# Eight stores to DRAM issued from GpSimd's queue instead of SyncE's, in a training step of an S4 convolution and a gated feed-forward layer

## The chip, the cores and the metric

The kernel runs on one core of a Trainium2 chip. The metric is the device time of one execution in microseconds (us). A kernel is executed several times and the median of its runs is quoted with the lowest and the highest. Ratios are computed as the mean time of one kernel's fast runs over that of the other's of the same rounds, so they are not quite the ratio of the medians that I quote. A run counts as slow when it is more than 1.5% above the fastest of the same kernel; slow runs are named where they matter. The kernel before was run on five different chips. Its medians ranged from 763.9 to 768.8 us and its single runs from 759.9 to 776.9 us (the last a slow run), so a difference of half a per cent between two kernels is not resolved. Each kernel was profiled once, in one of its runs, so stretches of two kernels are compared on one profile each.

## The reference

The function is a layer norm, a long convolution whose filter comes from a diagonal state-space model, a feed-forward layer, and a gate. The kernel computes the output and, for a given output gradient, the gradients of 11 inputs. Everything is bfloat16, with L = 2048 tokens, D = 512 channels, N = 128 states and F = 1792 hidden features.

```python
xn = _layernorm(x)
# _A_ref: K[d, l] = Re(sum_n C[d,n] * dB[d,n] * exp(l * dt[d] * A[d,n])), then an FFT convolution
s = irfft(rfft(xn, 2L) * rfft(K, 2L))[:L] + xn * Dskip
# _B_ref
o = silu(xn @ w1) @ w2
out = x + s * silu(o)
# outputs: out and the vjp of it for grad_out with respect to
# A_u, A_A_re, A_A_im, A_B_re, A_B_im, A_C_re, A_C_im, A_log_dt, A_Dskip, B_w1, B_w2
```

## The kernel before

Channels are handled in four blocks of 128 (`b` = 0 to 3). The FFT is done as two steps of matrix products with a transposing load, here called dB, between them. So each transform is a chain: TensorE, a copy on ScalarE, the transposing load (issued by SyncE), TensorE again.

```python
def dft_fwd(k, w8, U, ev, tag="w8"):
    # ... first step: TensorE products into ps, ev() casts them into A (dA) on ScalarE
    B = w8.tile([P, 2, 16, P], BF16, name="dB", tag=tag)
    nc.sync.dma_start_transpose(B[:]..., A[:]...)            # line 278: 1 MB, transposing
    for _ in range(LAG):
        yield                                                # other work is woven in here
    # ... second step: ps_s <- dB, F on TensorE (lines 287 and 288)
```

The backward stretch weaves three things: the transforms of the gradient, one block after the other; the feed-forward layer's gradient; and the output.

```python
def gen_ffn_da(k, da):
    for c in range(T // 2):                                  # 8 groups of 256 tokens
        dT = da.tile([P, 8, P], BF16, name="doT", tag="doT", bufs=2)
        nc.sync.dma_start_transpose(dT[:], k.do[...])        # line 845, "d o transpose"
        if c == 0:
            nc.sync.dma_start_transpose(k.W1T[:], k.ins["B_w1"])
        for f in range(FT // 2):
            if f in (0, 4):
                # ... slope <- Hd (line 855), Silu and Tanh on ScalarE, slope_less_one on VectorE
            # ... ps_da on TensorE; dh = (dh + 1) * ps_da on VectorE (line 867)
            if f in (3, 6):
                nc.sync.dma_start(k.DHd[...], dh[:, 0:n])    # line 870: store of d h, 512 or 384 KB
        for t in range(2):
            pd = da.tile([P, D], BF16, name="pd_s", tag="pd_s", bufs=1)
            # ... ps_dx on TensorE, cast on ScalarE
            nc.sync.dma_start(k.Pd[:, 2 * c + t, :], pd[:])  # line 879: store of partial d x, 128 KB
# gen_conv_bwd ends with
    nc.sync.dma_start(k.dUd[b], du[:]...)                    # line 648: store of d u
# gen_out stores the output from GpSimd already: k.st = nc.gpsimd.dma_start
```

The order in which each engine issues its instructions is not the order of this text. It is decided when the program is built, by a scheduler that works from its own idea of how long things take. Moving a store to another engine can therefore change the order of what comes later, on every engine. When the two programs are built and compared, TensorE, VectorE, ScalarE, GpSimd and SyncE all issue in another order, although the change touches no instruction of the first three.

Of the kernel before, what the change touches and what calls it, by code (L numbers as in the profile page):

```python
# [386 lines left out]
def gen_tables(k, b):  # L387

    nc, tbl = k.nc, k.tbl
    TT = nc.vector.tensor_tensor  # L390
    NX = NE + len(Y_EXP)
    Xr = tbl.tile([P, 4, NE, 32], BF16, name="Xr", tag="Xr")
    for h in range(2):
        hs = slice(b * P + 64 * h, b * P + 64 * h + 64)
        mag = tbl.tile([P, NX, 64], BF16, name="mag", tag="mag")
        nc.sync.dma_start(mag[:].rearrange("p e d -> p (e d)"), k.Md[2 * b + h])
        E = tbl.tile([P, 2, 16, NE, 4], BF16, name="E", tag="E", bufs=2)
        Y = k.Y[h]
        H = tbl.tile([P, 2, 16, 3, 4], BF16, name="H", tag="H")
        qe = lambda ap: ap.rearrange("p e (q a) -> p e q a", a=4)  # L400
        for (x0, n) in ((0, 8), (8, 8), (16, 5), (21, 7), (28, 3)):
            V = tbl.tile([P, 2, 8, 64], I32, name="V", tag="tv", bufs=2)
            TS = nc.vector.tensor_single_scalar
            TT(out=V[:, 1, 0:n], in0=k.tau[:, hs].unsqueeze(1).to_broadcast([P, n, 64]),
               in1=k.ecst[:, x0:x0 + n].unsqueeze(2).to_broadcast([P, n, 64]), op=ALU.mult)
            TS(out=V[:, 0, 0:n], in_=V[:, 1, 0:n], scalar=-float(1 << (PB - 2)), op=ALU.add)
            TS(out=V[:, :, 0:n], in_=V[:, :, 0:n], scalar=32 - PB, op=ALU.logical_shift_left)
            sn = tbl.tile([P, 2, 8, 64], BF16, name="sn", tag="ts", bufs=2)
            nc.scalar.activation(out=sn[:, :, 0:n], in_=V[:, :, 0:n], func=ACT.Sin, scale=-2 * PI_LO / 2.0 ** 32)
            for c in range(2):  # L410
                if x0 < NE:
                    segs = [(E[:, c, :, x0:x0 + n, :], 0, n)]
                else:
                    segs = [(Y[:, c, :, 1:8, :] if x0 == NE else H[:, c], 0, n)]
                for o, s0, s1 in segs:
                    TT(out=o.rearrange("p q e a -> p e q a"), in0=qe(sn[:, c, s0:s1]), in1=qe(mag[:, x0 + s0:x0 + s1, :]), op=ALU.mult)
            yield
        nc.sync.dma_start(k.Ed[b, h], E[:].rearrange("p c q e a -> p (c q e a)"))
        lo = lambda c: Y[:, c, :, 0:8, :].unsqueeze(2).to_broadcast([P, 16, 3, 8, 4])
        hi = lambda c: H[:, c].unsqueeze(3).to_broadcast([P, 16, 3, 8, 4])  # L420
        out = lambda c: Y[:, c, :, 8:32, :].rearrange("p q (k m) a -> p q k m a", m=8)
        shp = [P, 16, 3, 8, 4]
        for c, (x, y), op in ((0, ((0, 0), (1, 1)), ALU.subtract), (1, ((0, 1), (1, 0)), ALU.add)):
            m1 = tbl.tile(shp, BF16, name="m1", tag="tv", bufs=2)
            m2 = tbl.tile(shp, BF16, name="m2", tag="tm", bufs=1)
            TT(out=m1[:], in0=lo(x[0]), in1=hi(x[1]), op=ALU.mult)
            TT(out=m2[:], in0=lo(y[0]), in1=hi(y[1]), op=ALU.mult)
            TT(out=out(c), in0=m1[:], in1=m2[:], op=op)  # L428
        nc.sync.dma_start(k.Yd[b, h], Y[:].rearrange("p c q j a -> p (c q j a)"))
        yield  # L430
        for q0 in range(0, 16, 8):
            W = tbl.tile([P, 4, 8, NE, 4], BF16, name="W", tag="W", bufs=2)
            for m, (cm, ec) in enumerate(((0, 0), (1, 1), (2, 1), (1, 0))):
                d0 = hs.start + 4 * q0
                ct = k.CT[:, cm, d0:d0 + 32].rearrange("p (q a) -> p q a", a=4).unsqueeze(2).to_broadcast([P, 8, NE, 4])
                TT(out=W[:, m], in0=E[:, ec, q0:q0 + 8], in1=ct, op=ALU.mult)
            for u in range(2):
                ps = k.pt.tile([P, 4, 84], F32, name="ps_k", tag="pt")
                for q in range(4):
                    for m in range(4):  # L440
                        nc.tensor.matmul(out=ps[:, q], lhsT=Y[:, m // 2, q0 + 4 * u + q].rearrange("p j a -> p (j a)"),  # L441
                                         rhs=W[:, m, 4 * u + q].rearrange("p e a -> p (e a)"), start=(m == 0), stop=(m == 3))
                qq = 16 * h + q0 + 4 * u
                k.evk(Xr[:, :, :, qq:qq + 4], ps[:].rearrange("p q (e a) -> p a e q", a=4))
            yield

    def group(o, terms):
        n = len(terms) * 4
        i = 0
        for kind, e0, e1 in terms:  # L450
            for a in range(4):
                nc.tensor.matmul(out=o, lhsT=k.SEL[:, kind, a], rhs=Xr[:, a, e0:e1, :], start=(i == 0), stop=(i == n - 1))
                i += 1
    KE = tbl.tile([P, 8, 8, 32], BF16, name="KE", tag="KE")
    bc = lambda ap, n: ap.unsqueeze(2).to_broadcast([P, ap.shape[1], n, 32])
    ev = k.evk
    A = k.pt.tile([P, 16, 32], F32, name="ps_e", tag="pt")
    group(A[:], [(0, 0, 16)])
    ev(KE[:, 0], A[:, 8:16])
    ev(KE[:, 1:8, 0:2, :], bc(A[:, 0:7], 2))  # L460
    ev(KE[:, 2:8, 2, :], A[:, 1:7])
    ev(KE[:, 4:8, 3, :], A[:, 3:7])
    B = k.pt.tile([P, 16, 32], F32, name="ps_e", tag="pt")
    group(B[:, 0:5], [(0, 16, 21)])
    group(B[:, 5:12], [(1, 0, 7), (2, 1, 8)])
    group(B[:, 12:16], [(3, 3, 7), (2, 4, 8)])
    ev(KE[:, 1, 2, :], B[:, 0])
    ev(KE[:, 1, 3:6, :], B[:, 1:2].to_broadcast([P, 3, 32]))
    ev(KE[:, 1, 6, :], B[:, 2])
    ev(KE[:, 1, 7, :], B[:, 5])  # L470
    ev(KE[:, 2:4, 3:6, :], bc(B[:, 3:5], 3))
    ev(KE[:, 2:8, 6:8, :], bc(B[:, 6:12], 2))
    ev(KE[:, 4:8, 5, :], B[:, 8:12])
    ev(KE[:, 4:8, 4, :], B[:, 12:16])
    for a in range(4):
        nc.scalar.dma_start(k.Kd[b, a].rearrange("i j r -> j i r"), KE[a:P:4].rearrange("p i t q -> p i (t q)"))
    yield
# [8 lines left out]
def gen_conv_x(k, b):  # L486

    bs = slice(b * P, b * P + P)
    dft = k.dft
    U, _ = yield from dft_fwd(k, dft, lambda t: k.xn[:, t, bs], k.evc)  # L490
    k.nc.sync.dma_start(k.Ud[b], U[:].rearrange("p c g k -> p (c g k)"))
    yield


def gen_conv_fwd(k, b):

    nc, dft = k.nc, k.dft
    bs = slice(b * P, b * P + P)
    Kb = dft.tile([P, 4, 16, 32], BF16, name="Kb", tag="t4")
    nc.sync.dma_start(Kb[:].rearrange("p a t q -> p a (t q)"), k.Kd[b].rearrange("a i (r s) x -> (i r) a (s x)", s=2))  # L500
    for _ in range(LAG):
        yield
    KX, A2 = yield from dft_fwd(k, dft, lambda t: Kb[:, :, t, :], k.evc)
    U = spectrum_in(k, dft, b, "U")
    nc.sync.dma_start(k.KXd[b], KX[:].rearrange("p c g k -> p (c g k)"))
    yield
    cplx_mul(k, dft, KX, U)
    S = dft.tile([P, 16, P], BF16, name="S_b", tag="t4")

    def consume(t0, n, ps):  # L510
        xd = dft.tile([P, 8, P], BF16, name="xd", tag="cm2")
        nc.vector.tensor_tensor(out=xd[:], in0=k.xn[:, t0:t0 + n, bs], in1=k.Dbc[:, bs].unsqueeze(1).to_broadcast([P, n, P]), op=ALU.mult)
        nc.vector.tensor_tensor(out=S[:, t0:t0 + n], in0=ps[:], in1=xd[:], op=ALU.add)
    yield from dft_inv(k, A2, U, k.evc, consume)
    k.S_b = S
    nc.sync.dma_start(k.Sd[b], S[:].rearrange("p t d -> p (t d)"))
    yield


# [98 lines left out]
def gen_conv_bwd(k, b):  # L618
    nc, dft = k.nc, k.dftb
# [4 lines left out]
    U = spectrum_in(k, dft, b, "U")  # L624
    KX = spectrum_in(k, dft, b, "K")
# [15 lines left out]
    du = dft.tile([P, 16, P], BF16, name="du_b", tag="t4")  # L641
# [3 lines left out]
        TT(out=xd[:], in0=k.ds[:, t0:t0 + n, bs], in1=k.Dbc[:, bs].unsqueeze(1).to_broadcast([P, n, P]), op=ALU.mult)  # L645
        TT(out=du[:, t0:t0 + n], in0=ps[:], in1=xd[:], op=ALU.add)
    yield from dft_inv(k, A2, KX, k.evc, consume_dx)
    nc.sync.dma_start(k.dUd[b], du[:].rearrange("p t d -> p (t d)"))
    yield


# [187 lines left out]
def gen_ffn_da(k, da):  # L839
    nc = k.nc  # L840
    D, FT, DK, T = k.D, k.FT, k.DK, k.T
    W2T = k.W2T
    for c in range(T // 2):
# [6 lines left out]
        for f in range(FT // 2):  # L850
            if f in (0, 4):
                n = 8 if f == 0 else 6
                sl = da.tile([P, 8, 256], BF16, name="slope", tag="slope", bufs=2)
                dh = da.tile([P, 8, 256], BF16, name="dhT", tag="dhT", bufs=3)
# [12 lines left out]
            nc.vector.scalar_tensor_tensor(out=dh[:, i0:i0 + 2, :], in0=dh[:, i0:i0 + 2, :], scalar=1.0, in1=ps[:], op0=ALU.add, op1=ALU.mult)  # L867
            if f in (3, 6):
                f0, n = (0, 8) if f == 3 else (8, 6)
                nc.sync.dma_start(k.DHd[f0:f0 + n, :, 256 * c:256 * c + 256].rearrange("f p n -> p f n"), dh[:, 0:n])  # L870
            yield
        for t in range(2):
            pd = da.tile([P, D], BF16, name="pd_s", tag="pd_s", bufs=1)
# [2 lines left out]
                nc.tensor.matmul(out=ps[:], lhsT=dhs[ft // 8][:, ft % 8, t * P:t * P + P], rhs=k.W1T[:, ft, :],  # L876
                                 start=(ft == 0), stop=(ft == FT - 1))
            k.evb(pd[:], ps[:])
            nc.sync.dma_start(k.Pd[:, 2 * c + t, :], pd[:])
            yield  # L880


# [210 lines left out]
```

## Time and profile before

| Kernel before | |
|---|---|
| time, median (lowest to highest), 3 runs | 767.86 us (766.88 to 769.71) |
| span of the profiled run, mean granted TensorE clock | 767.7 us, 0.906 |
| first load of d o, the gate's input, issued (the forward part is nearly done) | 242.7 us |
| first d o transpose issued | 329.0 us |
| last store of d h issued | 519.9 us |
| first load for the weight gradients (GE) issued | 541.4 us |

The times of issue are read from the timeline and the line view of the trace. They cut the run into stretches that I use throughout: forward, the chain from the gate to the first d o transpose, the backward stretch from there to the last store of d h, and the rest.

The first lines are from the page of the kernel before: busy us of an engine, its share of the span and its instructions; then, for the two main DMA queues, packets, MB, and the share of 16 engines' time. q1 is fed by SyncE, q0 by GpSimd.

```profile
PE 581.8 (76%) x4987; PEld 405.3 (53%) x5036; DVE 547.6 (71%) x1110; ACT 494.9 (64%) x678; POOL 89.6 (12%) x167
...
DMA packets 262094, 167.32 MB, mean 218 GB/s; under 512 B 188816, under 2 KB 242064, under 8 KB 258192
...
q1 hardware_dynamic: 249056, 143.94, 74.1%
q0 software_dynamic: 6224, 18.10, 7.3%
```

No engine is full. (In the instruction counts a few TensorE records are missing from the trace.) The next lines are the kernel before by stretches: the window, its length, busy us and instruction count of each engine, granted clock, DMA share and GB/s.

```profile
core 0: us, PE busy (x) PEld busy (x) DVE busy (x) ACT busy (x) POOL busy (x), PEclk, DMA share, GB/s
50.00:245.00 195.00, 168.80 (x1520) 113.31 (x1539) 156.76 (x326) 159.45 (x241) 19.65 (x26) 0.95 0.81 234
245.00:335.00 90.00, 46.31 (x372) 31.94 (x374) 73.67 (x97) 50.38 (x65) 20.99 (x16) 0.77 0.90 258
335.00:515.00 180.00, 154.29 (x1234) 108.74 (x1246) 140.06 (x200) 128.22 (x128) 6.96 (x12) 0.95 0.82 224
```

TensorE is nearly full in the forward and backward stretches (169 of 195 us, 154 of 180 us) and half empty between them, where a chain of loads and gate arithmetic decides.

### The profile page before, as it was taken

To read this page: it belongs to the slowest core of one execution; us is meant where nothing else is said; L and a number is where in the kernel's file an instruction comes from. 1 tells how busy PE (TensorE), PEld (TensorE's weight loads), DVE (VectorE), ACT (ScalarE), POOL (GpSimd) and SP (SyncE) were. 2 spreads that over 40 slices of the span, in tenths; PEclk is the share of its full clock that TensorE was granted. 3 is DMA by queue.
4 is the path that set the end of the run, shared out by engine and by line. 5 is a ranking of instruction groups with operands and counts; after the bars stand their busy time and mean duration, and the time that the engine had idled before them with its cause. 6 is when DMAs were issued, how large, how long until landed. Compare 5 with 4: busy or idle time off the path is not lost. (4 is left out here: it accounts for less than half of the span.)

```text
span 767.7 us, 12970 instructions
## 1 busy us (share of the span) xinstructions
PE 581.8 (76%) x4987; PEld 405.3 (53%) x5036; DVE 547.6 (71%) x1110; ACT 494.9 (64%) x678; POOL 89.6 (12%) x167
## 2 busy tenths in 40 slices
PE   0579877888997616568887988995576877799995
PEld 0346653664763513356565575762263455488774
DVE  6979987685887985885796796877354293698620
ACT  6869767787998655476686587756365566474221
POOL 3020110010010351000000010001000002111220
PEclk9979988999999766999999899999589988899998
DMA  9988978499589759999969788289899999769373
GB/s 278 329 177 257 252 224 257 145 274 277 196 223 300 298 164 237 286 296 315 237 203 270 217 225 211 76 221 280 222 131 212 221 218 210 160 116 182 89 179 56
DMA packets 262094, 167.32 MB, mean 218 GB/s; under 512 B 188816, under 2 KB 242064, under 8 KB 258192
## 3 DMA queue, kind: packets, MB, share of 16 engines
q1 hardware_dynamic: 249056, 143.94, 74.1%
q0 software_dynamic: 6224, 18.10, 7.3%
q10 hardware_dynamic: 6752, 4.46, 2.0%
q8 instruction: 39, 0.64, 0.4%
q14 instruction: 23, 0.19, 0.1%
HBM read 58.06 MB, written 62.26 MB: 157 GB/s over the span
## 5 line engine op out<-in xcount | busy, mean ns | idle before, releaser
L42 ACT CAST dA<-ps_s 128x1024 bf16<-128x1024 f32 x96 | 94.3, 1030 | 37.7 <-PE ps_s L288 19.1
L537 PE MATMUL ps_h<-XT,W 128*128 128x256 bf16 x448 | 61.7, 289 | 32.2 <-DMA XT<-xn 25.3
L891 PE MATMUL ps_w<-do,a_tok 128*128 128x512 bf16 x215 | 60.3, 436 | 24.1 <-ACT a_tok L888 17.0
L537 PEld LDWEIGHTS <-W 128*128 128x128 bf16 x448 | 45.5, 104 | 43.4 <-issue 20.6
L717 DVE TENSOR_TENSOR Tp<-Vb,Eb 128x1344 bf16<-128x1344 bf16 x64 | 52.0, 852 | 20.4 <-PE psS L733 12.3
L300 PE MATMUL ps_i<-I,sp_in 128*128 128x256 bf16 x384 | 53.1, 285 | 16.1 <-DVE sp_in L323 9.4
L42 ACT CAST dB<-ps_i 128x1024 bf16<-128x1024 f32 x48 | 47.0, 1020 | 28.2 <-PE ps_i L300 22.7
L550 PE MATMUL ps_o<-W,aT 128*128 128x512 bf16 x210 | 56.8, 404 | 4.3 <-ACT aT L543 2.1
L287 PE MATMUL ps_s<-dB,F 128*128 128x512 bf16 x95 | 40.9, 431 | 22.9 <-DMA dB<-dA 19.7
L865 PE MATMUL ps_da<-doT,W2T 128*128 128x256 bf16 x448 | 55.4, 278 | 0.6 <-DVE dhT L867 0.5
L909 PE MATMUL ps_w<-dh_tok,xn 128*128 128x256 bf16 x448 | 53.8, 273 | 1.2 <-DMA dh_tok<-DHd 0.8
L876 PE MATMUL ps_dx<-W1T,dhT 128*128 128x512 bf16 x212 | 52.1, 379 | 3.2 <-DVE dhT L867 2.6
L300 PEld LDWEIGHTS <-sp_in 128*128 128x128 bf16 x384 | 37.3, 102 | 30.7 <-DVE sp_in L323 13.7
L891 PEld LDWEIGHTS <-a_tok 128*128 128x128 bf16 x224 | 23.3, 109 | 53.6 <-ACT a_tok L888 23.9
L865 PEld LDWEIGHTS <-W2T 128*128 128x128 bf16 x448 | 44.7, 100 | 10.0 <-issue 2.5
L42 ACT CAST o<-ps_w 128x256 bf16<-128x256 f32 (+1 forms) x42 | 18.5, 440 | 48.1 <-PE ps_w L909 33.5
L42 ACT CAST Vb<-ps_v 128x672 bf16<-128x672 f32 x64 | 42.7, 722 | 9.7 <-PE ps_v L707 9.4
L867 DVE SCALAR_TENSOR_TENSOR dhT<-dhT,ps_da 128x512 bf16<-128x512 bf16 x56 | 37.2, 682 | 14.9 <-PE ps_da L865 14.4
L909 PEld LDWEIGHTS <-xn 128*128 128x128 bf16 x448 | 42.6, 98 | 6.8 <-issue 2.4
L888 ACT ACTIVATE a_tok<-a_tok 128x2048 bf16<-128x2048 bf16 x14 | 26.7, 1910 | 28.3 <-DMA a_tok<-Hd 28.3
L275 PEld LDWEIGHTS <-TF 128*128 128x128 bf16 x384 | 26.5, 104 | 33.9 <-DMA Kb<-Kd 16.8
L441 PE MATMUL ps_k<-W,Y 128*128 128x84 bf16 x512 | 28.8, 213 | 13.8 <-DVE Y L428 10.1
(218 smaller groups left out, 1300.5 us busy)
## 6 DMA issues: line engine op xcount, KB each, us to landing
Yd<-Y SPq DMA_DIRECT2D x8, 1024.0 KB, 6.3
sp_in<-Ud SPq DMA_DIRECT2D x8, 1024.0 KB, 7.0
Ed<-E SPq DMA_DIRECT2D x8, 672.0 KB, 4.8
Eb<-Ed SPq DMA_DIRECT2D x8, 672.0 KB, 5.9
Hd<-hT POOLq DMA_DIRECT2D x8, 512.0 KB, 6.2
Ud<-dA SPq DMA_DIRECT2D x4, 1024.0 KB, 7.8
KXd<-dA SPq DMA_DIRECT2D x4, 1024.0 KB, 5.2
sp_in<-KXd SPq DMA_DIRECT2D x4, 1024.0 KB, 7.1
```

The lines of the kernel that those rows point to most:

```text
L42: return self.nc.scalar.copy(out=out, in_=in_)
L287: nc.tensor.matmul(out=ps[:, 4 * u:4 * u + 4], lhsT=F2[:, m0], rhs=B[:, 0, g0:g0 + 4, :], start=True, stop=False)
L300: nc.tensor.matmul(out=ps[:, g], lhsT=Y[:, c, g0 + g, :], rhs=k.I2[:, c].rearrange("p c m -> p (c m)"), start=(c == 0), stop=(c == 1))
L441: nc.tensor.matmul(out=ps[:, q], lhsT=Y[:, m // 2, q0 + 4 * u + q].rearrange("p j a -> p (j a)"), rhs=W[:, m, 4 * u + q].rearrange("p e a ...
L537: nc.tensor.matmul(out=ps[:, j], lhsT=k.W1[:, dk, ft * P:ft * P + P], rhs=XTv[:, :, dk, :], start=(dk == 0), stop=(dk == DK - 1))
L550: nc.tensor.matmul(out=ps[:], lhsT=aT[:, ft, t * P:t * P + P], rhs=k.W2[:, ft, :], start=(ft == 0), stop=(ft == FT - 1))
L717: k.nc.vector.tensor_tensor(out=Tp[:, c, :, r ^ c].rearrange("p e (q w) a -> p q w e a", w=2), in0=Vb[:, :, c].rearrange("p q w (e a) -> p ...
L865: nc.tensor.matmul(out=ps[:, j], lhsT=W2T[:, dk, ft * P:ft * P + P], rhs=dTv[:, :, dk, :], start=(dk == 0), stop=(dk == DK - 1))
L867: nc.vector.scalar_tensor_tensor(out=dh[:, i0:i0 + 2, :], in0=dh[:, i0:i0 + 2, :], scalar=1.0, in1=ps[:], op0=ALU.add, op1=ALU.mult)
L876: nc.tensor.matmul(out=ps[:], lhsT=dhs[ft // 8][:, ft % 8, t * P:t * P + P], rhs=k.W1T[:, ft, :], start=(ft == 0), stop=(ft == FT - 1))
L891: nc.tensor.matmul(out=ps[:], lhsT=a[:, t, :], rhs=k.do[:, t, :], start=(t == 0), stop=(t == k.T - 1))
L909: nc.tensor.matmul(out=ps[:], lhsT=k.xn[:, t, dk * P:dk * P + P], rhs=dh[:, t].rearrange("p j n -> p (j n)"), start=(t == 0), stop=(t == k ...
```

## The change

The change touches eight lines, which issue 64 stores in one execution. The intent is to keep loads from standing behind stores. SyncE issues in order, so a store whose data is not ready holds up all later loads. GpSimd's queue is almost empty.

```diff
-        nc.sync.dma_start(k.Ed[b, h], ...)      # tables E
+        k.st(k.Ed[b, h], ...)                   # k.st = nc.gpsimd.dma_start
-        nc.sync.dma_start(k.Yd[b, h], ...)      # tables Y
+        k.st(k.Yd[b, h], ...)
-    k.nc.sync.dma_start(k.Ud[b], ...)           # spectrum U
+    k.st(k.Ud[b], ...)
-    nc.sync.dma_start(k.KXd[b], ...)            # spectrum KX
+    k.st(k.KXd[b], ...)
-    nc.sync.dma_start(k.Sd[b], ...)             # s
+    k.st(k.Sd[b], ...)
-    nc.sync.dma_start(k.dUd[b], ...)            # d u
+    k.st(k.dUd[b], ...)
-                nc.sync.dma_start(k.DHd[...], dh[:, 0:n])    # d h
+                k.st(k.DHd[...], dh[:, 0:n])
-            nc.sync.dma_start(k.Pd[:, 2 * c + t, :], pd[:])  # partial d x
+            k.st(k.Pd[:, 2 * c + t, :], pd[:])
```

The first five I call the forward stores and the last three the backward stores. The change is in line with an advice of the Trainium skill ("Perfetto Trace Analysis", DMA Optimizations), which says of inputs and outputs, for loops and control flow above all, that "it may make sense to assign one DMA-capable engine to inputs (HBM→SBUF) and another to outputs (SBUF→HBM)".

More of the change, by code (lines that the diff above doesn't have):

```diff
@@ L417, in gen_tables @@
             yield
-        nc.sync.dma_start(k.Ed[b, h], E[:].rearrange("p c q e a -> p (c q e a)"))
+        k.st(k.Ed[b, h], E[:].rearrange("p c q e a -> p (c q e a)"))
         lo = lambda c: Y[:, c, :, 0:8, :].unsqueeze(2).to_broadcast([P, 16, 3, 8, 4])
@@ L428, in gen_tables @@
             TT(out=out(c), in0=m1[:], in1=m2[:], op=op)
-        nc.sync.dma_start(k.Yd[b, h], Y[:].rearrange("p c q j a -> p (c q j a)"))
+        k.st(k.Yd[b, h], Y[:].rearrange("p c q j a -> p (c q j a)"))
         yield
@@ L490, in gen_conv_x @@
     U, _ = yield from dft_fwd(k, dft, lambda t: k.xn[:, t, bs], k.evc)
-    k.nc.sync.dma_start(k.Ud[b], U[:].rearrange("p c g k -> p (c g k)"))
+    k.st(k.Ud[b], U[:].rearrange("p c g k -> p (c g k)"))
     yield
@@ L504, in gen_conv_fwd @@
     U = spectrum_in(k, dft, b, "U")
-    nc.sync.dma_start(k.KXd[b], KX[:].rearrange("p c g k -> p (c g k)"))
+    k.st(k.KXd[b], KX[:].rearrange("p c g k -> p (c g k)"))
     yield
@@ L515, in gen_conv_fwd @@
     k.S_b = S
-    nc.sync.dma_start(k.Sd[b], S[:].rearrange("p t d -> p (t d)"))
+    k.st(k.Sd[b], S[:].rearrange("p t d -> p (t d)"))
     yield
@@ L647, in gen_conv_bwd @@
     yield from dft_inv(k, A2, KX, k.evc, consume_dx)
-    nc.sync.dma_start(k.dUd[b], du[:].rearrange("p t d -> p (t d)"))
+    k.st(k.dUd[b], du[:].rearrange("p t d -> p (t d)"))
     yield
@@ L869, in gen_ffn_da @@
                 f0, n = (0, 8) if f == 3 else (8, 6)
-                nc.sync.dma_start(k.DHd[f0:f0 + n, :, 256 * c:256 * c + 256].rearrange("f p n -> p f n"), dh[:, 0:n])
+                k.st(k.DHd[f0:f0 + n, :, 256 * c:256 * c + 256].rearrange("f p n -> p f n"), dh[:, 0:n])
             yield
```

## The prediction

> **What bounds it now.** No single engine. The page's busy line: TensorE 76%, VectorE 71%, ScalarE 64%, GpSimd 12%; its queue table: the DMA engines 84% (SyncE's queue 74%). In the table by stretches, 50 to 245 us (forward) has TensorE busy 169 of 195 us, 335 to 515 us (backward) 154 of 180. Between them TensorE is busy 46 of 90 us: a latency chain. After 515 us only stores already on GpSimd remain.
>
> **What moves.** 64 stores (8 tables E, 8 Y, 4+4 spectra, 4 s, 4 d u, 16 d h, 16 partial d x; about 34 MB) leave SyncE. The order listing also shows another order of the other engines' work. Bytes and DMA engines stay; the Trainium skill ("DMA: Bandwidth & Descriptors", Issuing engines are not separate DMA queues) says that all issuers share the same 16 engines and only sequencer issue time is saved.
>
> *Removed:* 64 issues of 0.32 to 0.39 us (about 23 us of SyncE), and SyncE's waits for a store's data, holding up loads behind it; in the queue's waits 25 us at Y, 19 at E, 22 at d h, 15 at partial d x, 11 at s, 10 at d u: about 103 us.
> *Added:* 64 GpSimd issues of 0.56 to 0.9 us (as h and its output now): about 45 us on an engine 12% busy. Landing is later: 512 KB stores land in 6.2 us from GpSimd, 4.7 from SyncE.
>
> **How much is on the critical path.** Little. In SyncE's timeline the transposes of the DFT waited for their own input; TensorE's waits for DMA in the forward and backward stretches are about 20 us in all: 0 to -4 us. GpSimd now has the head-of-line waits; h is double buffered, so a few us there don't reach ScalarE.
>
> In the chain after 245 us, the load of Kb stands behind a store of s and a load (issued 281.0, its data written by about 276.5): -4.5 us. But in the new order the 12 us transpose load of W1T stands ahead of the DFT transposes instead of after them: these go from 293 to about 300 us, and d o's transpose, held to 329 us by W1T today, is ready at about 331. Net +2 to +4 us.
>
> From 507 to 556 us SyncE issues almost without a gap and TensorE idles about 20 us for a_tok and GE. Some 8 us of store issues and waits go; two prefetches of d h (2.8 us each) move ahead of GE, one a_tok (4.4 us) behind it: -3 to -6 us.
>
> Sum: about -3 us, give or take 1% for the new order.
>
> **Predicted: 765 us, 8 in 10 between 751 and 780. Faster 0.13, within 2% 0.75, slower 0.12.**
>
> **What would show it.** DMA bytes as before, GpSimd busy about 135 us; SyncE's waits much shorter, the stores' waits now under GpSimd; forward and backward stretches within 4 us of 195 and 180; Kb issued earlier and the first DFT transpose behind W1T; GE issued about 5 us sooner after the last d h store.
>
> **What would make it wrong.** Loads no longer share a ring with stores and overtake them, so transposes land clearly faster: faster. Or GpSimd's in-order queue blocks: partial d x has one buffer, so its store stuck behind an output store stops ScalarE, then TensorE; or the gate's arithmetic on GpSimd (21 us, about 260 to 292) waits behind a store of s: slower.

## More of the kernel before

What TensorE waits for in the backward stretch is in the view of waits (total us, times, longest us):

```profile
engine line waited for: us in total, times, longest us
PE ps_s L287 <- DMA dB<-dA: 11.2, 3, 5.1
```

So the one wait of size there is for the transposing load dB, three times. SyncE's timeline around the second of these (start, us, what was issued) shows how the loads and stores share one queue:

```profile
413.07 6.98 SPq L278 DMA_TRANSPOSE dB<-dA  x1
420.14 0.53 SPq L879 DMA_DIRECT2D Pd<-pd_s  x1
...
423.62 0.39 SPq L870 DMA_DIRECT2D DHd<-dhT  x1
```

Issuing dB holds SyncE for 7 us. Every store that became ready in that time is issued behind it.

## The result, and the profile after

The changed kernel takes 791.49 us (790.96 to 794.53, 4 runs) against 768.79 us (766.88 to 771.61, 4 runs) of the kernel before in the same rounds. The ratio is 1.030 with a 95% interval of 1.0257 to 1.0344. It is slower. The span of the profiled run is 789.2 us, and the granted clock 0.893.

The same lines of the changed kernel's page:

```profile
PE 587.1 (74%) x5036; PEld 408.0 (52%) x5036; DVE 547.1 (69%) x1110; ACT 493.3 (63%) x678; POOL 129.4 (16%) x231
...
DMA packets 248014, 167.32 MB, mean 212 GB/s; under 512 B 188816, under 2 KB 225680, under 8 KB 244112
...
q1 hardware_dynamic: 227552, 108.03, 60.3%
q0 software_dynamic: 13648, 54.01, 19.7%
```

The bytes are the same; 36 MB have moved from q1 to q0, and GpSimd works 40 us more. The same fixed windows, first columns as before:

```profile
50.00:245.00 195.00, 165.43 (x1506) 111.00 (x1504) 153.56 (x315) 154.23 (x235) 29.48 (x41) 0.94 0.77 225
245.00:335.00 90.00, 42.69 (x294) 26.53 (x293) 63.93 (x89) 49.13 (x64) 24.86 (x23) 0.67 0.94 273
335.00:515.00 180.00, 146.81 (x1159) 100.85 (x1158) 134.50 (x193) 118.21 (x121) 25.22 (x39) 0.92 0.78 204
```

TensorE, VectorE and ScalarE do less in the same time in all three, at a clock that is lower too. Where the 21.5 us of span came from:

| us | before | after | difference |
|---|---|---|---|
| start to first load of d o | 242.7 | 249.1 | +6.4 |
| to first d o transpose | 86.3 | 92.7 | +6.4 |
| to last store of d h (backward stretch) | 190.9 | 197.4 | +6.5 |
| to first GE load | 21.5 | 23.0 | +1.5 |
| to the end | 226.3 | 227.0 | +0.7 |

The wait that grew in the backward stretch, in the changed kernel's view of waits:

```profile
PE ps_s L287 <- DMA dB<-dA: 20.4, 3, 12.6
```

TensorE waits 20.4 us for dB instead of 11.2. The timeline of the changed kernel around its second dB there, SyncE first and then GpSimd:

```profile
433.10 7.42 SPq L278 DMA_TRANSPOSE dB<-dA  x1
...
434.54 0.90 POOL L870 DMA_DIRECT2D DHd<-dhT  x1 [2.04 <-DVE dhT L867]
437.21 0.55 POOL L614 DMA_DIRECT2D out_dram<-go_x  x1 [1.77 <-DVE go_x L613]
438.40 0.84 POOL L870 DMA_DIRECT2D DHd<-dhT  x1 [0.64 <-DVE dhT L867]
```

Both stores of d h are now issued while dB is in flight. The DMA view of the changed kernel over that flight (433.1 to 449.3 us) gives KB and the us from issue to landing:

```profile
DMA packets 6256, 3.42 MB, mean 211 GB/s; under 512 B 4225, under 2 KB 5812, under 8 KB 6256
...
DHd<-dhT POOLq DMA_DIRECT2D x1, 512.0 KB, 12.4
DHd<-dhT POOLq DMA_DIRECT2D x1, 384.0 KB, 11.2
...
out_dram<-go_x POOLq DMA_DIRECT2D x1, 256.0 KB, 11.7
...
dB<-dA SPq DMA_TRANSPOSE x1, 16.2
```

dB takes 16.2 us to land, and everything in flight beside it is slow too. The three dB of the backward stretch land in 10.5, 16.2 and 7.5 us here, against 9.4, 10.3 and 8.4 us before.

### The profile page after: what moved, and what is told of

The parts are those of the page before. It is cut to its first block, busy times and chain, and to the rows that moved or that the text cites. A ratio compares the mean times of both kernels' runs of the same rounds, so it can differ in the third digit from the quotient of the medians.

```text
span 789.2 us, 13075 instructions
## 1 busy us (share of the span) xinstructions
PE 587.1 (74%) x5036; PEld 408.0 (52%) x5036; DVE 547.1 (69%) x1110; ACT 493.3 (63%) x678; POOL 129.4 (16%) x231
## 2 busy tenths in 40 slices
DMA packets 248014, 167.32 MB, mean 212 GB/s; under 512 B 188816, under 2 KB 225680, under 8 KB 244112
## 4 chain that ended last, share of the span: by engine, by line
issue 29%; DVE 18%; DMA 18%; PE 17%; ACT 7%; POOL 6%; SPq 4%; POOLq 0%; ACTq 0%; DVEq 0%
DMA dB<-dA 4%; DMA a_tok<-Hd 4%; PE ps_dx L876 3%; DVE Tp L717 2%; PE ps_w L891 2%; DMA G<-in_grad_out_dram 2%; PE ps_i L300 2%; PE ps_da L865 2%; SPq L904 1%; POOL Hd L544 1%; DMA slope<-Hd 1%; PE ps_o L550 1%; DMA Od<-ob 1%; DMA out_dram<-go_x 1%; DVE g_t L751 1%
## 5 line engine op out<-in xcount | busy, mean ns | idle before, releaser
L287 PE MATMUL ps_s<-dB,F 128*128 128x512 bf16 x96 | 42.2, 440 | 39.5 <-DMA dB<-dA 36.8
L891 PE MATMUL ps_w<-do,a_tok 128*128 128x512 bf16 x224 | 57.4, 408 | 16.7 <-ACT a_tok L888 16.7
L300 PE MATMUL ps_i<-I,sp_in 128*128 128x256 bf16 x384 | 55.0, 291 | 18.3 <-DVE sp_in L323 13.0
L537 PEld LDWEIGHTS <-W 128*128 128x128 bf16 x448 | 45.4, 103 | 42.0 <-issue 18.9
L550 PE MATMUL ps_o<-W,aT 128*128 128x512 bf16 x224 | 58.8, 405 | 3.8 <-ACT aT L543 2.5
L876 PE MATMUL ps_dx<-W1T,dhT 128*128 128x512 bf16 x224 | 54.1, 381 | 1.6 <-DVE dhT L867 1.6
L320 DVE TENSOR_TENSOR cm<-sp_in,dA 128x1024 bf16<-128x1024 bf16 x24 | 16.5, 689 | 47.8 <-ACT dA L42 31.8
L288 PE MATMUL ps_s<-dB,F 128*128 128x512 bf16 x96 | 41.6, 433 | 0.0
```

The costliest lines, as they stand in the source:

```text
L287: nc.tensor.matmul(out=ps[:, 4 * u:4 * u + 4], lhsT=F2[:, m0], rhs=B[:, 0, g0:g0 + 4, :], start=True, stop=False)
L288: nc.tensor.matmul(out=ps[:, 4 * u:4 * u + 4], lhsT=F2[:, m1], rhs=B[:, 1, g0:g0 + 4, :], start=False, stop=True)
L300: nc.tensor.matmul(out=ps[:, g], lhsT=Y[:, c, g0 + g, :], rhs=k.I2[:, c].rearrange("p c m -> p (c m)"), start=(c == 0), stop=(c == 1))
L537: nc.tensor.matmul(out=ps[:, j], lhsT=k.W1[:, dk, ft * P:ft * P + P], rhs=XTv[:, :, dk, :], start=(dk == 0), stop=(dk == DK - 1))
L550: nc.tensor.matmul(out=ps[:], lhsT=aT[:, ft, t * P:t * P + P], rhs=k.W2[:, ft, :], start=(ft == 0), stop=(ft == FT - 1))
L876: nc.tensor.matmul(out=ps[:], lhsT=dhs[ft // 8][:, ft % 8, t * P:t * P + P], rhs=k.W1T[:, ft, :], start=(ft == 0), stop=(ft == FT - 1))
```

## The experiments

Two things changed at once, the queue and the issue order. To separate them I pinned each engine's order: a list of the traced instructions is added to the program, and each instruction is chained to the one before it on its engine by a dependency that only fixes the order and adds no wait. Called "old order" is the order of the kernel before, "changed order" that of the changed kernel. The edit common to all the pinned kernels is this:

```diff
+ORDER = "..."    # packed list: position of each instruction in the traced program
+def pin(nc, tc):
+    info = mybir.DependencyInfo(mybir.DependencyClass.NoSync, ...)
+    for j in ORDER:                                   # cut: unpacking
+        ins = traced[j]
+        if ins.engine in last: tc.add_manual_dep(ins, last[ins.engine], info, ...)
+        last[ins.engine] = ins.name
```

When the pinned kernels are built again and compared with the two originals, every engine issues in the order that the text says. A kernel pinned to its own order was not timed; the nearest to such a control is fwd_gpsimd_old_order below, at 0.9996. All outputs are right. Each line of measurement gives the median (lowest to highest) of 4 runs and the ratio to the kernel before of the same rounds, with its 95% interval.

### Queue alone, order alone, and the place of W1T

My first theory was that the new order was at fault, through W1T: its 12 us transposing load had moved ahead of the transforms, as the prediction had noted. The rival was the queue itself.

```diff
 gpsimd_old_order:     the changed kernel's stores   + pin to the old order
 synce_new_order:      the kernel before's stores    + pin to the changed order
 w1t_late_new_order:   the changed kernel, changed order, but in SyncE's order
-  ... S, S, W1T, dB, dB, U, ... d o transpose, d o transpose
+  ... S, S, dB, dB, U, ... d o transpose, d o transpose, W1T
 w1t_early_old_order:  the kernel before, old order, but W1T ahead of the first of these dB
```

> The 64 stores on GpSimd, but every engine issues in the order that the kernel before has (pinned by order-only edges; the stores take their old places among GpSimd's own instructions). Theory Order (the slowdown comes from the other order of issue that the compile-time scheduler chose once the stores had moved): 760 to 772 us, within 1% of before. Theory Queue (the slowdown comes from issuing on GpSimd: later landing, shared rings, in-order waits there): 785 to 795 us.

Measured: 762.21 us (756.15 to 773.84), 0.9898 (0.9815 to 0.998); its profiled run was a slow one (773.84 us), so its stretches are not compared with fast ones. In this order the queue alone has no cost that is resolved.

> The 64 stores stay on SyncE, but every engine issues in the order of the changed kernel. Theory Order: 785 to 800 us, as slow as the changed kernel or a little slower since SyncE's head-of-line waits come on top. Theory Queue: 765 to 772 us.

Measured: 777.42 us (773.03 to 779.59), 1.0115 (1.0046 to 1.0184). The order alone costs about 1.2%. Its first d o transpose comes at 341.9 us, as late as in the changed kernel, but its backward stretch is 182.8 us.

> The changed kernel with its own order, except that the transposing load of W1T is issued behind the first two transposes of d o instead of ahead of the DFT transposes. If W1T's place alone costs the stretch after the forward part its 6 us and more: 779 to 786 us, with the first DFT transpose issued at about 294 instead of 304 us and the first d o transpose at about 330 instead of 342. If something else delays these transposes: 789 to 794 us.

Measured: 798.0 us (794.43 to 803.63), 1.0375 (1.0296 to 1.0453), slower than the 794 us of the rival. The first d o transpose still comes at 342.9 us, and the backward stretch, which needs W1T, is 209.1 us. W1T stood behind two d o transposes here, while in the kernel before it is ahead of them.

> The kernel before with its own order, except that W1T's load is issued ahead of the first DFT transpose, as in the changed kernel. If W1T's place costs what the changed kernel lost there: 774 to 780 us. My prediction's arithmetic (d o's transpose was held by W1T anyway) says 768 to 772 us.

Measured: 775.15 us (767.76 to 776.35), 1.0072 (0.9996 to 1.0149); the first d o transpose came at 327.6 us. The median lies in the range expected if W1T's place costs, but the run profiled is the fastest of the four, and the other three (774.6 to 776.4 us) left no profile. So a cost of W1T's place of up to 1.5% in the old order is not excluded. But W1T's place is not what makes the first d o transpose late: with W1T ahead it came at 327.6 us in the old order, with W1T behind at 342.9 us in the changed one. What stands out instead is that order alone is +1.2%, queue alone -1.0%, and both are +3.0%: they don't add, and the surplus is in the backward stretch, 197.4 us against 182.8.

### Which stores carry the backward loss

Theory A: on their own queue the backward stores overtake dB and share the DMA engines with it. With the stores on SyncE in the changed order, the DMA view of synce_new_order over the flight of the same second dB (423.8 to 433.8 us) reads:

```profile
DMA packets 5927, 2.82 MB, mean 282 GB/s; under 512 B 4208, under 2 KB 5644, under 8 KB 5927
...
DHd<-dhT SPq DMA_DIRECT2D x1, 512.0 KB, 4.1
...
dB<-dA SPq DMA_TRANSPOSE x1, 10.0
```

dB lands in 10.0 us, and the d h store, which SyncE could issue only after dB's 7.5 us of issuing, in 4.1 us. TensorE's wait for dB in this kernel is:

```profile
PE ps_s L287 <- DMA dB<-dA: 9.9, 3, 5.6
```

The kernels that test theory A all pin the changed order, or for the fourth the old one, and differ in which stores are on GpSimd.

```diff
 fwd_gpsimd_new_order, fwd_gpsimd_old_order (from the changed kernel):
-    k.st(k.dUd[b], ...)  /  k.st(k.DHd[...], ...)  /  k.st(k.Pd[...], ...)
+    nc.sync.dma_start(...)                           # all three
 dh_synce_new_order (from the changed kernel):
-                k.st(k.DHd[...], dh[:, 0:n])
+                nc.sync.dma_start(k.DHd[...], dh[:, 0:n])
 dh_only_gpsimd_new_order (from the kernel before):
-                nc.sync.dma_start(k.DHd[...], dh[:, 0:n])
+                k.st(k.DHd[...], dh[:, 0:n])
```

> The issue order of the changed kernel is pinned; the five forward and table stores stay on GpSimd, the three backward ones (d u, d h, partial d x) go back to SyncE. Theory A (contention: with their own queue the backward stores overtake and share the DMA engines with the transposing loads dB that TensorE waits for): time 774 to 782 us, the dB landings of the backward stretch back from 10.5, 16.2 and 7.5 us to about 7.3, 10.0 and 7.1, TensorE's wait for dB there from 20.4 to about 10 us, the stretch from the first d o transpose to the last store of d h from 197 to about 183 us. Rival B (the forward stores on GpSimd are what costs, through the places they take): time stays at 788 to 794 us.

Measured: 773.6 us (771.22 to 775.65), 1.0121 (1.0035 to 1.0207). The dB landings are 7.3, 11.6 and 7.5 us, TensorE's wait for them 12.4 us, and the backward stretch 186.5 us.

> The changed kernel with its order pinned, only the store of d h (the largest of the backward stores) back on SyncE. Theory A (contention by bytes): most of the backward loss returns, 776 to 785 us, second dB landing under 12 us. Rival C (partial d x's single buffer and the in-order GpSimd queue behind it cost): nearly no change, 788 to 793 us, since partial d x and d u stay on GpSimd.

Measured: 775.16 us (770.25 to 779.83), 1.0132 (1.0044 to 1.0219). With d h alone back on SyncE the landings are 8.8, 9.3 and 7.8 us, and the backward stretch is 186.7 us: this one store returns as much as all three did (186.5 us). Some 4 us to the 182.8 us of synce_new_order remain, which one profile each does not resolve. Rival C falls, since partial d x and d u had stayed on GpSimd. Its lines for the second dB's flight (427.9 to 437.2 us):

```profile
DMA packets 5982, 2.51 MB, mean 270 GB/s; under 512 B 4193, under 2 KB 5757, under 8 KB 5982
...
dB<-dA SPq DMA_TRANSPOSE x1, 9.3
```

> The changed order is pinned; only the store of d h is on GpSimd, the seven other stores are on SyncE. Complement of dh_synce_new_order (775 us). Theory A with d h's store as the carrier: the stretch from the first d o transpose to the last store of d h at 193 to 198 us, the second dB landing of the backward stretch over 12 us, time 784 to 792 us. If it takes the combination of stores, the stretch stays at 183 to 188 us and the time at 775 to 780 us.

Measured: 789.78 us (787.12 to 796.87), 1.0291 (1.0181 to 1.0401). This is the complement: d h alone on GpSimd brings most of the loss back, 195.4 us in the backward stretch against 182.8 with all stores on SyncE and 197.4 with all on GpSimd. Its waits and its second flight (428.6 to 446.9 us):

```profile
PE ps_s L287 <- DMA dB<-dA: 21.6, 3, 13.9
```

```profile
DMA packets 6040, 3.66 MB, mean 200 GB/s; under 512 B 4240, under 2 KB 5536, under 8 KB 6040
...
DHd<-dhT POOLq DMA_DIRECT2D x1, 512.0 KB, 14.2
DHd<-dhT POOLq DMA_DIRECT2D x1, 384.0 KB, 11.8
...
dB<-dA SPq DMA_TRANSPOSE x1, 18.3
```

One thing changed with d h's queue besides the time of issue, and it was not separated from it. The page of this kernel has these queue lines:

```profile
q1 hardware_dynamic: 234464, 136.60, 70.1%
q0 software_dynamic: 8272, 25.44, 10.5%
```

In synce_new_order, where d h is on SyncE, q1 has 249056 packets with 143.94 MB and q0 has 6224 with 18.10 MB, as in the kernel before. So the same 7.34 MB of d h go as 14,592 packets of about 0.5 KB from SyncE and as 2,048 of about 3.6 KB from GpSimd. Whether a d h store in small packets that overtook dB would slow it as much, no run shows.

> The order of the kernel before is pinned, only the five forward and table stores on GpSimd, the backward ones on SyncE. If theory A holds, the forward gain of the queue (about 1 to 3 us up to the first d o transpose) is kept and the backward stretch stays at about 191 us: 757 to 765 us, at or below the 762 us of all eight stores on GpSimd in that order. If the backward stores on GpSimd were a gain, it is 765 to 770 us.

Measured: 764.64 us (761.5 to 768.15), 0.9996 (0.9919 to 1.0074). In the old order the forward stores gain nothing that can be resolved.

### Why the old order does not suffer

gpsimd_old_order_2 is the same kernel as gpsimd_old_order, run again. pd2_gpsimd_old_order is that with a second buffer for partial d x, the risk that my prediction had named.

```diff
-            pd = da.tile([P, D], BF16, name="pd_s", tag="pd_s", bufs=1)
+            pd = da.tile([P, D], BF16, name="pd_s", tag="pd_s", bufs=2)
```

> The same kernel as gpsimd_old_order (all eight stores on GpSimd, order of the kernel before), again, for a profile of a fast run: its first profile was of its slowest run (772 us). Expected 758 to 765 us, 0.5 to 1.5% under the kernel before; dB landings of the backward stretch longer than in the kernel before by 1 to 3 us each, if theory A (contention with the backward stores) holds in this order too; then the forward part must be shorter by more than that.

Measured: 769.29 us (763.74 to 770.49), 1.0023 (0.9954 to 1.0093). The backward stretch is 190.9 us, as in the kernel before, and the dB landings there are 9.4, 10.4 and 8.9 us. In GpSimd's timeline of this kernel only one store of d h falls into the second dB's flight, 418.0 to 428.4 us, and it comes late in it, 6.3 us after dB (in the changed kernel the two came after 1.4 and 5.3 us):

```profile
424.34 1.40 POOL L870 DMA_DIRECT2D DHd<-dhT  x1 [3.31 <-DVE dhT L867]
```

TensorE's wait for dB in the backward stretch is no longer than before:

```profile
PE ps_s L287 <- DMA dB<-dA: 8.3, 2, 4.9
```

So the queue has no resolved cost in an order that keeps two d h stores from flying beside one dB. The expectation that landings would lengthen by 1 to 3 us each was wrong in this run. Over all the fast profiles with the old backward order it holds weakly: the second dB lands in 10.4 to 11.9 us with d h on GpSimd (four) and in 9.0 to 10.3 us with d h on SyncE (four).

> The same with two buffers for partial d x. Theory G (its single buffer, held by a store in GpSimd's in-order queue, stalls ScalarE for about 15 us in the backward stretch): ScalarE's wait for the store of partial d x goes from 15 us to under 2, and the time falls 1 to 5 us below that of gpsimd_old_order_2. Rival: the wait is slack and nothing changes.

Measured: 774.67 us (770.65 to 775.55), 1.0097 (1.0033 to 1.0161). ScalarE's wait for the store of partial d x, 9.0 us in the run above, is gone from the longest waits, but the kernel is not faster. In its profile TensorE's wait for dB is 15.2 us instead of 8.3, so whether that wait was slack or its gain was lost again at dB stays open.

### The late first d o transpose

In the changed order the first d o transpose comes some 10 to 15 us later than the 329.0 us of the kernel before (338.9 to 344.1 us in ten profiles), whichever queue the stores take. SyncE's timeline in this stretch, kernel before:

```profile
280.50 0.33 SPq L566 DMA_DIRECT2D G<-in_grad_out_dram  x1
280.99 0.38 SPq L500 DMA_DIRECT2D Kb<-Kd  x1
281.47 10.17 SPq L1050 DMA_TRANSPOSE W2T<-in_B_w_dram  x4
...
292.85 5.91 SPq L278 DMA_TRANSPOSE dB<-dA  x1
298.80 0.57 SPq L482 DMA_DIRECT2D sp_in<-Ud  x1
```

and the changed kernel:

```profile
277.24 0.38 SPq L500 DMA_DIRECT2D Kb<-Kd  x1
277.79 10.89 SPq L1050 DMA_TRANSPOSE W2T<-in_B_w_dram  x4
292.94 0.33 SPq L566 DMA_DIRECT2D G<-in_grad_out_dram  x1
...
294.27 9.69 SPq L848 DMA_TRANSPOSE W1T<-in_B_w_dram  x1
304.07 10.03 SPq L278 DMA_TRANSPOSE dB<-dA  x2
314.21 0.51 SPq L482 DMA_DIRECT2D sp_in<-Ud  x1
```

It is tempting to read the cause off these lines: G, W1T and the load of U each sit in a new place. Moving them, one and all, tested that. G and U went back to their old places; W1T went behind two d o transposes, so further back than in the kernel before.

```diff
 u_early_gpsimd (changed kernel, changed order):
-  ... dB, dB, U, ...
+  ... dB, U, dB, ...
 chain_fix_gpsimd (in addition; chain_fix_fwd_gpsimd also has the backward stores on SyncE):
-  ... Kb, W2T x4, G, S, S, W1T, dB, ...   d o transpose, d o transpose
+  ... G, Kb, W2T x4, S, S, dB, ...        d o transpose, d o transpose, W1T
```

> The changed kernel with its order pinned, but the load of spectrum U of the last forward block moved ahead of the transposing load of d s's dB, as it was before. Theory D (in the changed order that load sits behind a transposing load that waits for the gate arithmetic and ScalarE, which delays the last product, the last s and the first d o transpose): the first d o transpose at about 330 us after the start instead of 341.8, the product's wait for U from 14 us to under 8, time 778 to 784 us. Rival E (TensorE and VectorE order delays it anyway): first d o transpose stays later than 338 us, time 787 to 793 us.

Measured: 786.43 us (782.44 to 790.74), 1.0281 (1.0197 to 1.0365). The first d o transpose is at 341.2 us and the product still waits 10.0 us for U (14.1 in the changed kernel), so theory D falls.

> The changed kernel with its order pinned, and three loads of SyncE's queue put back where they were in the kernel before: the last load of G ahead of Kb and W2T's transposing loads, U's load ahead of the second transposing load dB, and W1T behind the first two transposing loads of d o. W1T late alone, and U early alone, left the first d o transpose at 342.9 and 341.2 us. Theory F (the three are in series in one in-order queue, so that each alone only uncovers the next): the first d o transpose at 329 to 335 us, time 778 to 784 us; the backward stretch stays long (about 197 us). Rival E (the order of the compute engines holds it): later than 338 us, time 786 us or more.

Measured: 800.52 us (796.95 to 802.29), 1.0439 (1.0372 to 1.0506). The first d o transpose is at 344.1 us, so theory F falls as well. G waited in SyncE's queue until 293 us for its buffer, and Kb, which was behind it, now made TensorE wait 22.4 us, against 7.4 in the changed kernel and 16.6 in the kernel before. This suggests that G was late because the gate, which frees its buffer, was late, and not the other way round.

> The same, and the three backward stores back on SyncE. If both causes are right and add up, the first d o transpose is at 329 to 335 us, the stretch to the last store of d h about 183 to 186 us, and the time 760 to 768 us, which is at or below the kernel before.

Measured: 782.66 us (781.98 to 786.77), 1.0229 (1.0151 to 1.0306), with the first d o transpose at 342.5 us and a backward stretch of 194.6 us, so the expectation failed in all three. Against chain_fix_gpsimd, which differs in the backward stores' queue alone, it is 18 us faster; 12.4 us of this are in the backward stretch (207.0 there).

Since moving single loads failed, I joined the two orders at a point: all instructions before a chosen one in one order, the rest in the other. Putting the compute engines in one order and the DMA queues in the other was not possible; both such mixtures deadlocked in the build and were not run.

```diff
 old_then_new_synce, old_then_new_gpsimd: pin to old order up to the first d o transpose, changed order after it
 new_then_old_gpsimd:                     pin to changed order up to the first d o transpose, old order after it
 new_to_220us_synce:                      pin to changed order up to the dB that starts at about 221 us, then old
 new_to_gate_gpsimd:                      pin to changed order up to the first load of d o, then old
```

> All stores on SyncE; the issue order of the kernel before up to the first d o transpose, that of the changed kernel after it. If the changed order's loss lies wholly before that point and its backward part is better on SyncE (182.8 us against 190.9), the first d o transpose is at about 329 us, the stretch after it 182 to 186 us and the time 758 to 764 us, under the kernel before. If the backward stretch owes its 182.8 us to the late start (loads already there), it is 190 us and the time 766 to 770 us.

Measured: 769.94 us (768.07 to 772.81), 1.0063 (1.0012 to 1.0115). The first d o transpose is at 332.4 us, and the backward stretch 189.6 us. So the 182.8 us of synce_new_order came with its late start, and the changed backward order is no better by itself.

> The same order with all eight stores on GpSimd. Theory A (stores that overtake share the DMA engines with the transposing loads TensorE waits for, where the changed backward order puts them side by side): first d o transpose at about 330 to 333 us, the stretch after it 193 to 198 us, dB landings of over 10 us, time 774 to 782 us. If it stays at the level of the run above, the queue's cost needs the changed forward order too and theory A is wrong.

Measured: 780.09 us (776.44 to 785.72), 1.0177 (1.0113 to 1.0241). The first d o transpose is at 336.3 us, later than expected. The backward stretch is 201.1 us, dB landings are 10.7, 15.8 and 8.1 us. TensorE's wait for dB, in the run above and in this one:

```profile
PE ps_s L287 <- DMA dB<-dA: 10.2, 3, 5.7
...
PE ps_s L287 <- DMA dB<-dA: 18.3, 3, 12.2
```

The queue's cost in the backward stretch needs the changed backward order and not the changed forward order, as theory A says.

> All eight stores on GpSimd; the changed order up to the first d o transpose, the order of the kernel before after it. If the two stretches' costs add up: the first d o transpose at 341 to 344 us, the stretch after it about 191 us (as with all stores on GpSimd in the old order), time 780 to 785 us.

Measured: 777.78 us (776.22 to 778.99), 1.0161 (1.0113 to 1.021). The first d o transpose is at 341.6 us, the backward stretch 190.5 us. The time is 2 us under the expected range. The late d o transpose and the long backward stretch can thus be switched on one without the other.

> All stores on SyncE; the changed order up to the transposing load dB that starts at about 221 us, the old order after it. In the kernels with the changed order the dB at 221 us came 4 to 6 us late and the first d o transpose 12 us late. If the loss has two independent parts, the d o transpose is at 333 to 336 us and the time 770 to 775 us; if all of it comes from the part after 221 us, it recovers to about 330 us and 768 us.

Measured: 770.77 us (768.42 to 780.78, the last a slow run), 1.0061 (0.9998 to 1.0123). The first d o transpose is at 331.4 us, so about 10 of the 12 us arise after the dB of about 221 us.

> All eight stores on GpSimd, the changed order up to the load of d o's first half (the start of the gate), the old order from there. With the changed order up to the first d o transpose that one came at 341.6 us, with it up to the dB at 221 us at 331.4 us, in the old order at 329 to 333 us. If the loss lies in the forward feed-forward part between 221 us and the gate, the d o transpose stays at 340 to 343 us; if it lies in the gate and the last convolution, it comes at 331 to 334 us; if both share it, at 335 to 339 us. The stretch after it about 191 us, so the time 770 to 780 us.

Measured: 777.15 us (771.62 to 778.54), 1.0083 (0.9996 to 1.0169). The first d o transpose is at 335.1 us. Of the 10 us between new_to_220us_synce and new_then_old_gpsimd, some 4 lie before the gate's start and 6 after it. This is coarse: the first of these kernels has its stores on SyncE and the other two on GpSimd, and the old order with all stores on GpSimd put that transpose at 327.6 us in one profile (of a slow run) and at 333.3 in another. The backward stretch is 194.2 us. Which engine's order holds it in either part stays open.

## Why the prediction was wrong

The backward stretch, by order and queue, in us from the first d o transpose to the last store of d h:

| | d h on SyncE | d h on GpSimd |
|---|---|---|
| old backward order | 190.9 (before), 190.0 (fwd_gpsimd_old_order), 193.5 (w1t_early_old_order), 189.0 (new_to_220us_synce) | 190.9 (gpsimd_old_order_2), 193.8 (pd2_gpsimd_old_order), 190.5 (new_then_old_gpsimd), 194.2 (new_to_gate_gpsimd) |
| changed backward order, early start | 189.6 (old_then_new_synce) | 201.1 (old_then_new_gpsimd) |
| changed backward order, late start | 182.8 (synce_new_order), 186.5 and 186.7 (forward stores, or all but d h, on GpSimd) | 197.4 (after), 195.4 (only d h on GpSimd), 193.3 (u_early_gpsimd) |
| the same, W1T behind two d o transposes | 194.6 (chain_fix_fwd_gpsimd) | 207.0 (chain_fix_gpsimd), 209.1 (w1t_late_new_order) |

The slow profile of gpsimd_old_order (199.0) is left out. In the old order the two columns overlap; in the changed order they lie 6.6 us or more apart in every row.

Taking the profiled spans, the 21.5 us divide into 8.5 us for the order (synce_new_order, 776.2, over before, 767.7) and 13.0 us for the queue in that order (after, 789.2, over synce_new_order). The ratios, 1.2% for the order and 3.0% for both, agree with this.

- **"Forward and backward stretches: 0 to -4 us" was the step that failed.** I took the waits for DMA as an upper bound on what could change, and supposed that the transfers themselves would take as long as before. In the backward stretch they did not: dB's second landing went from 10.0 to 16.2 us, and TensorE's wait for dB from 9.9 to 20.4 us (synce_new_order and after, same order). That 10.5 us is most of the 14.6 us by which the stretch grew; another 2.6 us is TensorE being busy longer (162.8 and 165.4 us, at a granted clock of 0.98 and 0.94), and the rest is not accounted for. Against the kernel before, the stretch grew by 6.5 us. The forward part failed too: the first load of d o came 6.4 us later instead of up to 4 us earlier. This goes with the order, since with the stores on SyncE in the changed order it came 10.8 us later (253.5 us); why is open.
- **The overtaking was foreseen, with the wrong sign.** I wrote that loads and stores no longer sharing a ring would let transposing loads land clearly faster. What overtook was the stores. While SyncE issued dB for 5 to 7.5 us, a store on the same queue had to stay behind it; on GpSimd it went out at once and shared the engines. Two runs show that the store of d h carries this: taking it alone back recovers most of the backward loss (186.7 us), moving it alone brings most of it on (195.4 us). That it does so by overtaking fits all runs, but d h's packets also grew from 0.5 to 3.6 KB with the change of queue, and the two were not tested apart. Sharing the engines doesn't explain the size either. In the second flight the engines were as busy as on SyncE but moved 211 GB/s instead of 282 (DMA share 1.12 and 1.13 in the view by windows), and I have no run that says why.
- **The other two named risks were not the cause.** The single buffer of partial d x does make ScalarE wait when its store is on GpSimd in the old order (9.0 us), but in the changed kernel's backward stretch that wait is 1.0 us, and a second buffer in the old order gained nothing. The gate's arithmetic did not wait long behind a store of s: GpSimd stood 2.6 us at that store (at 280.2 us), and the first d o transpose was as late with all stores on SyncE.
- **The chain was mis-sized: +2 to +4 us predicted.** The d o transpose came at 341.8 us, not 331; half of these 12.8 us arose before the first load of d o, half in the chain itself (+6.4 us). Kb was earlier as predicted (277.2 against 281.0 us) and the first dB was behind W1T as predicted, but neither decided. The changed order costs about 12 us by then, on either queue, and about 10 of them arise after 221 us. What in that order holds the transpose up stays open. I had allowed "give or take 1% for the new order"; it was 1.2%, all in one direction.
- **The transition after 507 us: -3 to -6 us predicted, +1.5 us measured** from the last store of d h to the first GE load. No experiment was spent on it. (The prediction has it that after 515 us only stores already on GpSimd remained; in the kernel before, the last stores of d h and of partial d x left SyncE at 519.9 and 528.3 us.)
- **Right:** the bytes stayed at 167.32 MB, GpSimd was busy 129 us (135 predicted), and in the old order the queue alone changes nothing resolved (0.990 and 1.002). That is near the predicted sum of -3 us, but its parts were not confirmed there: the backward stretch was 190.9 us as before and the transition 21.0 us against 21.5. The stores' waits did move to GpSimd (54.3 us at d h). No kernel beat the kernel before beyond the scatter of these repeats.

Three places of the Trainium skill bear on this. The page "DMA: Bandwidth & Descriptors" (Issuing engines are not separate DMA queues) says that all issuers end on the same 16 engines and that using several saves sequencer time only. The equal bytes agree with it, but I read it as meaning that the landing of dB doesn't depend on who issues the stores, and it does. The same page (Queues, rings and completion order) says that each DMA engine takes turns between the queue rows that have work, a packet at a time. The slow flights, with stores in larger packets, fit that, since dB (16.2 us) and the stores beside it (12.4 and 11.2 us) were all slow; no run here shows the turns themselves. The page "Advanced Engine Details and Errata" (X-Bar Transpose (TRN2)) says that transposing transfers are as fast as regular ones. This trace agrees only in part: in the kernel before dB, 1 MB, landed in 6.7 to 10.6 us (median 9.1), and a plain 1 MB load of a spectrum in 5.4 to 10.0 (median 7.0). With two of the d h stores on GpSimd beside it, it took 13.4 to 18.9 us in the six kernels that have them there.

## What to carry to other kernels

A shared in-order queue is not only a cost: a store that must wait until a long load has been issued meets only the end of that load's flight, so before moving a store ask which load that an engine waits for it will now fly beside. When a build-time scheduler orders the program, a change of queue is also a change of order; pin the order and test the two apart before explaining either. Don't mend an order by moving the loads that look late, since they may be late for the same reason as everything else; swap whole stretches first to see where the delay arises.

## What the Trainium skill lacked or had wrong

- "Perfetto Trace Analysis" (DMA Optimizations) gives the advice to put inputs and outputs on different engines, for loops and control flow above all, without saying when it harms. Here it cost 3.0% in the kernel as built and nothing resolved (1.002) with the old order.
- "DMA: Bandwidth & Descriptors" (Issuing engines are not separate DMA queues) leaves out that changing the issuer lets a store overtake a load that it used to stand behind: the second backward dB landed in 16.2 us instead of 10.0, and in 18.3 us with d h alone moved.
- No page that I found says what rate is left when a transposing load and stores from GpSimd overlap. Here it was 211 and 200 GB/s in such flights, and 282 and 270 GB/s where the d h stores were behind the load.
- "DMA: Bandwidth & Descriptors" gives about 1 us from GpSimd to the first byte, but for the generation of descriptors there only "small, variable", and no figure for how long a store holds GpSimd. Here a d h store held GpSimd for 0.84 to 0.94 us in the changed kernel and SyncE for 0.39 us (median) in the kernel before; the medians of partial d x were 0.55 and 0.33 us.
